# Two q loads of the second batch issued before the weights, and the last block's statistics on a turn of their own, in a retention-then-Fourier-mixing kernel

## The chip, the cores and the metric

One core of one Trainium2 chip. The metric is the device time of one execution in microseconds. TensorE (PE in the profile) does the matmuls and writes PSUM; VectorE (DVE) and ScalarE (ACT) read PSUM and do the elementwise work; GpSimd (POOL) does elementwise work on SBUF and issues the weight loads; SyncE (SP) issues all other DMAs.

## What is computed

q, k, v are 4 batches x 8 heads x 768 positions x 64, in float32. The first half is a retention recurrence with one decay per head, the second a Fourier mixing with a normalised two-layer MLP:

```python
for t in range(S):
    state = gamma * state + einsum('bhd,bhe->bhde', k[:, :, t], v[:, :, t])
    y[:, :, t] = scale * einsum('bhd,bhde->bhe', q[:, :, t], state)
x = y.transpose(0, 2, 1, 3).reshape(B, S, H * D)            # 4 x 768 x 512
u = x + real(fft(fft(x, axis=1), axis=2))
un = (u - mean(u)) / sqrt(var(u) + 1e-06)                   # over the last axis
out = u + maximum(un @ w_ch1, 0.0) @ w_ch2                  # 512 -> 2048 -> 512
```

## The kernel before, in words

**Attention.** The recurrence is done in six chunks of 128 positions, two heads (a pair) at a time, so a batch has four pairs. For each pair q, k and v come by one DMA each of 384 KB (L191, in the first batch L211) into the pool `inp` of 11 buffers. They are cast to f16 (`cast_unit`, L411: q at L423, k with its decay at L433, v at L438, on POOL). q and k are transposed on TensorE (`t_unit`, L598, tile `tq`, L615) and copied back by ACT. `a_unit` (L651) makes the products of k and q (`wkA`, L659), which DVE masks into `atm` (L662); `kv_unit` (L668) makes the states (`wkK`, then `s`, L688); `y_unit` (L694) adds state part and in-chunk part (`wkY`, L709 and L713), and ACT writes x (L721).

**Mixing.** x is folded (`fold_*`), multiplied by the tables of the first transform (`s1_unit`, L835), then of the second (`s2_unit`, L985), which gives u in six blocks of 128 rows, numbered kb: DVE at L1011 and L1014 (L1026 and L1028 in the first batch), POOL adding x at L1032 and L1034. `norm_unit` (L1038) takes the row statistics of one block: `bn_stats` (tile `bst`, L1044) and `bn_aggr` (`stats`, L1045) on DVE, then the centred copy `un` on ACT (L1046). `unT_unit` transposes `un`, on TensorE or by DMA. `rstd_unit` takes the roots (L1056, L1058).

**MLP.** It runs per batch in two halves (rt 0 and 1) of three blocks. `h_unit` (L1077) makes one of 16 rows fb of 128 hidden units: four matmuls into `psh` (L1082), one of three PSUM buffers that `psc` shares, emptied through the ReLU into `ht16` by ACT (L1086) if fb stands in `ACT_ROWS`, else by DVE (L1088). `ch_unit` (L1114) follows with 16 matmuls per block into `psc` (L1125); DVE forms the output (L1129) and SP stores it. The first batch's rt=0 uses `h0_unit` (L1099).

**The order of the work.** All engines work in order. The first batch's attention follows a list written by hand, `FIRST` (L34): each word is one unit, with its engine after `@`; `w0` to `w7` are the eight weight loads that POOL issues (L1139, L1146). The kind `long` makes fillers of f32 (L174), a matmul of zeros that only keeps TensorE going. Nine f16 fillers (L166, called at L237) stand before the list. All later work is put into streams: a list of units with a begin and an end in units of one batch; `emit` (L1249) spreads each stream's units evenly over its interval and sorts all units by time. `mix_units` (L1239) gives the streams of one half's second transform: three turns of `s2_unit`, each with the `norm_unit` of the block before, the last turn also with its own block's. The times stand in `DM0`, `DM1`, `DA0`, `DA1` (L49 to L52). For the first batch alone, POOL's order is pinned to the order of emission. Within these streams a scheduler still places the instructions of each engine.

**The loads of the second batch** stand in a stream of their own (L1291) with `after` = 6: each waits for the seventh weight load to land and for a matmul of the first batch (L193), and SP stays at the first of them until then. Their order is q, k, v pair by pair. Behind them in SP's queue come the output stores and the DMA transposes of the second batch.

Where the steps touch TensorE's program: the second batch's first transposes of q and k (L615, between psc matmuls of the first batch), the wkY matmuls at L713, and the rows of psh in the last batch.

Of the kernel before, what the change touches and what calls it, by code (L numbers as in the profile page):

```python
# [31 lines left out]
LOADS0 = [("q", 0), ("k", 0), ("q", 1), ("k", 1), ("v", 0), ("k", 2), ("v", 1), ("q", 2), ("v",  # L32
          2), ("q", 3), ("k", 3), ("v", 3)]
FIRST = """  # L34
k00@a k01@a tsa0@v ts0 xe1 tsa4@g gk1@a q0 t00 tsa2@v ts2 ta02 e00@a tsa1@g ts4 t01 tsa3@g ts1
ta00 e01@a ta10 ta22 v00@g par@v q1 gk0@g k10@v k11@a ta12 am00 am01 ta42 ta11 k20@g ae010@v
ae001@v kv0 ae000@v ae011@v t10 sc0 t11 e10@a yi01 v10@g yi00 yx0 e11@a am10 q2 x01@a am11 ts3
ta32 ta20 x00@v ta01 fl4@g ae101@v ae100@v k21@a kv1 t20 ta21 e20@a ae111@v yi11 t21 sc1
ae110@v yi10 fs0 fl2@g yx1 q3 s110 k31@g e21@a x10@v am20 am21 x11@a fs1 ta40 v22@a s010 k30@a
# [9 lines left out]
DM0, DM1 = (0.183, 0.205, 0.286, 0.408), (0.004, 0.137, 0.232, 0.341)  # L49
# [4 lines left out]
HT0 = (0.666, 0.693, 0.632, 0.590)  # L54
NPE = 2
KD = (3,)
ACT_ROWS = ((2, 5, 6, 7, 8, 9, 10, 14), (0, 3, 6, 7, 9, 10, 11, 12, 14, 15), (2, 4, 5, 6, 7, 8, 10, 14))


@with_exitstack  # L60
def kernel(
# [104 lines left out]
    def filler(n):  # L166
        def run():
            for _ in range(n):
                nc.tensor.matmul(wps, wz[:, 0:P], wz, start=True, stop=True)
        return run  # L170
# [3 lines left out]
    def filler32(n):  # L174
        def run():
            for _ in range(n):
                nc.tensor.matmul(wps[:, 0:256], wz32[:, 0:P], wz32, start=True, stop=True)
        return run

    in_of, a_of = {}, {}  # L180
    w_dma = []
    srcs = {"q": q, "k": k, "v": v}

    def load_unit(b, i, after=None):
        def run():
            h0 = 2 * PAIR_ORDER[i]
            for name, src in srcs.items():
                t = inp.tile([P, 2, NCH, D], f32, tag="in32", name=f"{name}32")
                rows = "h (p c) d -> p h c d" if b < NPE and name == "q" else \
                    "h (c p) d -> p h c d"  # L190
                dma = nc.sync.dma_start(t, src[b, h0:h0 + 2].rearrange(rows, p=P))  # L191
                if after is not None:
                    for x in (w_dma[after].ins, lb[0]["mm"].ins):  # L193
                        tc.add_manual_dep(dma.ins, x.name,
                                          mybir.DependencyInfo(mybir.DependencyClass.Sync,
                                                               mybir.DependencyReason.DATA),
                                          reason="loads in turn")
                if b > 1:
                    tc.add_manual_dep(dma.ins, a_of[b - 1, 1].ins.name,
                                      mybir.DependencyInfo(mybir.DependencyClass.Sync,  # L200
                                                           mybir.DependencyReason.DATA),
                                      reason="loads behind the transposes")
                in_of[name, b, i] = t
        return run

    def first_load(name, i, eng):
        def run():
            h0 = 2 * ORD0[i]
            t = in_of[name, 0, i] = inp.tile([P, 2, NCH, D], f32, tag="in32", name=f"{name}32")
            rows = "h (p c) d -> p h c d" if name == "q" else "h (c p) d -> p h c d"  # L210
            eng.dma_start(t, srcs[name][0, h0:h0 + 2].rearrange(rows, p=P))  # L211
        return run

    for name, i in LOADS0:
        first_load(name, i, nc.sync)()


    icol_i = const.tile([P, 8], i32, tag="icol_i")
# [15 lines left out]
    nc.gpsimd.iota(icol_i[:, 5:6], pattern=[[0, 1]], base=127, channel_multiplier=-1)  # L234
    nc.gpsimd.iota(kf_i, pattern=[[1, KN]], base=0, channel_multiplier=0)
    nc.gpsimd.memset(wz, 0.0)
    filler(9)()  # L237
    for h in range(H):
        nc.vector.memset(lgrow[:, h:h + 1], float(lng[h]))
    nc.vector.memset(maskf, 1.0)  # L240
# [148 lines left out]
    for j in range(2):  # L389
# [6 lines left out]
        t = const.tile([P, 257], f32, tag=f"qn_{j}", name=f"qn_{j}", padded_shape=[P, 260])  # L396
# [641 lines left out]
    def norm_unit(b, kb):  # L1038
        def run():
            u, stats = lb[b]["u"], lb[b]["st"]  # L1040
            bst = stt.tile([P, 6], f32, tag=f"bst{kb % 3}", name="bst")
            un = unp.tile([P, 2, 257], f16, tag="un16", name="un16").rearrange(
                "p a b -> p (a b)")[:, 0:DM]
            nc.vector.bn_stats(bst, u[:, kb, :])  # L1044
            nc.vector.bn_aggr(stats[:, kb, 0:2], bst)  # L1045
            nc.scalar.activation(un, u[:, kb, :], AF.Identity, bias=stats[:, kb, 0:1], scale=-1.0)  # L1046
            lb[b]["un", kb] = un
        return run

    def rstd_unit(b, rt):  # L1050
        def run():
            stats = lb[b]["st"]
            if b == 0 and rt == 0:
                bn_unit(0)()
            sl = slice(3 * rt, 3 * rt + 3)
            nc.scalar.activation(stats[:, sl, 2:3], stats[:, sl, 1:2], AF.Sqrt, bias=epsT,  # L1056
                                 scale=1.0)
            nc.vector.reciprocal(out=stats[:, sl, 3:4], in_=stats[:, sl, 2:3])  # L1058
        return run

    def unT_unit(b, kb):
        def run():
            un, unT = lb[b].pop(("un", kb)), lb[b]["unT"]
            if b > 1 or b and kb >= 3:
                nc.sync.dma_start_transpose(unT[:, :, kb * P:(kb + 1) * P], un)
                return
            pst = ps_g.tile([P, 4, P], f16, tag="g", name="pst", padded_shape=[P, 8, P])
            for cb in range(4):
                nc.tensor.transpose(pst[:, cb, :], un[:, cb * P:(cb + 1) * P], ident16)
            if (kb % 2 == 0) != (b == 0 and kb < 3):  # L1070
                nc.vector.tensor_copy(unT[:, :, kb * P:(kb + 1) * P], pst)
            else:
                nc.scalar.copy(unT[:, :, kb * P:(kb + 1) * P], pst)
        return run


    def h_unit(b, rt, fb):  # L1077
        def run():
            unT = lb[b]["unT"]
            psh = ps_pm.tile([P, 384], f32, tag="pm", name="psh", padded_shape=[P, DM])  # L1080
            for cb in range(4):
                nc.tensor.matmul(psh, w116[:, cb, fb * P:(fb + 1) * P],  # L1082
                                 unT[:, cb, rt * 384:(rt + 1) * 384],
                                 start=(cb == 0), stop=(cb == 3))
            if fb in ACT_ROWS[2 if (b, rt) == (B - 1, 0) else rt]:
                nc.scalar.activation(ht16[:, fb, :], psh, AF.Relu, bias=0.0, scale=-1.0)  # L1086
# [149 lines left out]
                    s=s1b_unit, sa=sa_unit, bn=bn_unit, pt=pt0_unit,  # L1236
                    gr=gr_unit, xe=x_edges)[kind](*n)

    def mix_units(b, kbs):  # L1239
        def turn(j):  # L1240
            def run():
                if j < len(kbs):
                    s2_unit(b, kbs[j])()
                for n in kbs[max(j - 1, 0):j] + (kbs[-1:] if j == len(kbs) - 1 else []):
                    norm_unit(b, n)()
            return run
        return [turn(j) for j in range(len(kbs))], [unT_unit(b, kb) for kb in kbs]

    def emit(streams):  # L1249
        ev = []  # L1250
# [18 lines left out]
    streams = []  # L1269
    for b in range(B):  # L1270
        majors = []
        if b == 0:
            for kb in range(3):
                if kb:
                    majors.append(unT_unit(0, kb))
                majors += [h0_unit(kb, g) for g in range(4)]
        else:
            majors += [h_unit(b, 0, fb) for fb in range(NFB)]
        majors.append(rstd_unit(b, 0))
        majors += [ch_unit(b, 0, rb3, part) for rb3 in range(3) for part in range(4)]  # L1280
# [3 lines left out]
        s2s, unTs = mix_units(b, [3, 4, 5])  # L1284
        dm = DM0 if b == 0 else DM1
        streams += [(majors, b, b + 1.0), (s2s, b + dm[0], b + dm[1]),
                    (unTs, b + dm[2], b + dm[3])]
        if b + 1 < B:
            steps = attn_steps(b + 1)
            if b == 0:  # L1290
                streams.append(([load_unit(1, i, 6) for i in range(4)], LD0[0], LD0[1]))  # L1291
                streams.append(([qt_zeros], 0.1, 0.15))
                streams.append(([half_tables], HT0[0], HT0[1]))
                streams.append(([pad_unit], HT0[2], HT0[3]))
                ts = TS0
            else:
                streams.append(([load_unit(b + 1, i) for i in range(4)], b + LD1[0], b + LD1[1]))
                n = [len(u) for u in steps[1:]]
                ts = list(TS1[:2]) + [TS1[2] + TS1[3] * sum(n[:j]) / sum(n) for j in range(6)]
# [6 lines left out]
            s2s, unTs = mix_units(b + 1, [0, 1, 2])  # L1306
            streams += [(s2s, end + da[2], end + da[3]), (unTs, end + da[4], end + da[5])]
    emit(streams)


# [28 lines left out]
```

## Time and profile before

| | |
|---|---|
| median of 3 runs | 245.32 us (245.0 to 245.47) |
| the profiled execution | 245.19 us |
| its span, first to last instruction | 243.1 us |
| TensorE busy | 230.3 us (95%) |
| VectorE, ScalarE, GpSimd busy | 173.6, 120.7, 83.3 us |
| mean granted TensorE clock | 0.986 |
| moved by DMA | 36.59 MB, mean 151 GB/s |
| 16 loads each of q, k, v | 384 KB each, about 6 us to landing |
| 8 weight loads, cast to f16 on the way | 512 KB each as stored, 11.3 us to landing |

The time of the profiled execution is the span and about 2 us around it. A timeline row is: start, duration, engine, line and operation, output<-input, shape, count, and in brackets the idle time before it with what ended it. Where rows are merged, the duration is that of the group. Matmul ends are modelled: rows of TensorE overlap, so the starts say more than the ends. PEld rows are its weight loads. A row of stretches has the stretch, its length, the busy time (and count) of PE, PEld, DVE, ACT and POOL, the granted clock as a share of full speed, the DMA share (in these rows the mean over the 16 engines can read above 1, since packets overlap) and GB/s.

### The profile page before, as it was taken

The page shows a single profiled execution, that of the slowest core. Times are in us where ns is not written, and L with a number is a line of the kernel's source. Part 1 is how long each engine was busy: PE and PEld are TensorE (multiplying, and loading weights), DVE is VectorE, ACT ScalarE, POOL GpSimd, SP SyncE. Part 2 cuts the span into 40 slices and gives each one's busy share as a digit, 9 for nine tenths or more (in the row PEclk, how much of TensorE's full clock was granted, in tenths as well). Part 3 has the DMA queues.
Part 4 walks back from the last instruction along what each step waited for, and adds up shares of the span by engine and source line. Part 5 has one row for each costly group of instructions (what it writes and reads, how often), then busy time and mean ns, then how long its engine had stood idle before and what let it go on. Part 6 is the DMA issues. An engine that isn't in the chain of part 4 may idle for free.

```text
span 243.1 us, 5251 instructions
## 1 busy us (share of the span) xinstructions
PE 230.3 (95%) x2005; PEld 144.3 (59%) x2005; DVE 173.6 (71%) x423; ACT 120.7 (50%) x267; POOL 83.3 (34%) x151
## 2 busy tenths in 40 slices
PE   6399999989999999999999999899999999999994
PEld 1376679756865646665557446555675455446543
DVE  8979987947997889986985749977886557414121
ACT  5989758665865444841248406722356316203400
POOL 7678802356500097850001808920003214000000
PEclk9769999999999999999999999999999999999999
DMA  7996999999989859999999588775100230221012
GB/s 184 229 271 103 203 206 194 234 225 255 279 184 226 155 123 242 175 186 141 266 273 215 102 176 183 157 109 151 46 0 0 75 122 23 43 89 43 1 43 89
DMA packets 100009, 36.59 MB, mean 151 GB/s; under 512 B 90640, under 2 KB 97040, under 8 KB 99984
## 3 DMA queue, kind: packets, MB, share of 16 engines
q1 hardware_dynamic: 95760, 32.06, 63.3%
q0 software_dynamic: 4224, 4.19, 10.7%
q8 instruction: 16, 0.26, 0.5%
q14 instruction: 9, 0.07, 0.1%
HBM read 27.26 MB, written 6.29 MB: 138 GB/s over the span
## 4 chain that ended last, share of the span: by engine, by line
PE 68%; DVE 13%; DMA 5%; ACT 4%; POOL 4%; issue 2%; SPq 1%; POOLq 0%; ACTq 0%; DVEq 0%
PE psc L1125 32%; PE psh L1082 21%; DMA v<-in_v_dram 3%; PE ps L842 3%; PE wkA L659 2%; DMA k<-in_k_dram 2%; DVE atm L662 2%; DVE bst L1044 2%; PE wkY L713 2%; DVE u L1011 2%; POOL u L1032 1%; POOL u L1034 1%; DVE ht L1088 1%; PE ps L822 1%; PE pq L916 1%
## 5 line engine op out<-in xcount | busy, mean ns | idle before, releaser
L1125 PE MATMUL psc<-w,ht 128*128 128x512 f16 (+2 forms) x400 | 88.9, 370 | 0.0
L1082 PE MATMUL psh<-unT,w 128*128 128x384 f16 x448 | 81.8, 326 | 0.5 <-ACT ht L1086 0.3
L1125 PEld LDWEIGHTS <-ht 128*128 128x128 f16 x400 | 37.6, 98 | 36.8
L1082 PEld LDWEIGHTS <-w 128*128 128x128 f16 x448 | 42.3, 98 | 24.9 <-issue 1.9
L1086 ACT ACTIVATE ht<-psh 128x384 f16<-128x384 f32 x64 | 30.9, 490 | 42.2 <-PE psh L1082 41.5
L1032 POOL TENSOR_TENSOR u<-u,x 128x256 f32<-128x256 f32 x21 | 13.3, 635 | 105.7 <-DVE u L1011 93.3
L1129 DVE SCALAR_TENSOR_TENSOR ob<-psc,stats,u 128x512 f32<-128x512 f32 (+2 forms) x25 | 18.1, 725 | 29.6 <-PE psc L1125 29.5
L1088 DVE TENSOR_SCALAR ht<-psh 128x384 f16<-128x384 f32 x48 | 26.3, 550 | 8.9 <-PE psh L1082 8.3
L662 DVE TENSOR_TENSOR atm<-wkA,maskp 128x512 f16<-128x512 f32 x36 | 23.6, 680 | 1.7 <-PE wkA L659 1.6
L1046 ACT ACTIVATE un<-u,stats 128x512 f16<-128x512 f32 x21 | 14.7, 720 | 13.4 <-DVE stats L1045 8.5
L1044 DVE BATCH_NORM_STATS2 bst<-u 128x6 f32<-128x512 f32 x21 | 14.5, 691 | 5.6 <-POOL u L1034 5.4
L688 DVE SCALAR_TENSOR_TENSOR s<-s,gk,wkK 128x128 f16<-128x128 f16 x48 | 16.2, 337 | 2.6 <-ACT s L684 1.8
L721 ACT ACTIVATE x<-wkY,gexp 128x384 f16<-128x384 f32 x24 | 12.6, 579 | 8.9 <-PE wkY L713 8.9
L433 POOL TENSOR_SCALAR kd<-k,gexp 128x384 f16<-128x384 f32 x24 | 13.8, 585 | 3.3 <-DMA k<-in_k_dram 3.3
L659 PE MATMUL wkA<-qTz,kT 128*128 128x256 f16 x72 | 13.4, 272 | 0.0
L1034 POOL TENSOR_TENSOR u<-u,x 128x256 f32<-128x256 f32 x21 | 13.3, 635 | 0.0
L1006 ACT COPY qn<-pq 128x128 f32<-128x128 f32 x18 | 4.9, 274 | 14.0 <-PE pq L1004 13.9
L1099 PEld LDWEIGHTS <-w 128*128 128x128 f16 x192 | 11.0, 98 | 0.8 <-issue 0.3
L1099 PE MATMUL psh<-unT,w 128*128 128x128 f16 x192 | 11.4, 219 | 0.1
L1011 DVE SCALAR_TENSOR_TENSOR u<-pq,g,qn 128x256 f32<-128x256 f32 x18 | 8.5, 474 | 3.3 <-PE psh L1082 2.5
L438 POOL TENSOR_SCALAR v<-v 128x768 f16<-128x768 f32 x12 | 10.0, 831 | 1.1 <-DMA v<-in_v_dram 1.1
L659 PEld LDWEIGHTS <-kT 128*128 128x128 f16 x72 | 6.9, 98 | 5.6 <-issue 0.4
(177 smaller groups left out, 315.0 us busy)
## 6 DMA issues: line engine op xcount, KB each, us to landing
q<-in_q_dram SPq DMA_DIRECT2D x16, 384.0 KB, 6.0
k<-in_k_dram SPq DMA_DIRECT2D x16, 384.0 KB, 5.8
v<-in_v_dram SPq DMA_DIRECT2D x16, 384.0 KB, 6.2
out_dram<-ob SPq DMA_DIRECT2D x23, 256.0 KB, 2.8
w<-in_moe_w_ch_dram POOLq DMA_DIRECT2D x8, 512.0 KB, 11.3
unT<-un SPq DMA_TRANSPOSE x15, 2.4
out_dram<-ob SPq DMA_DIRECT2D x1, 192.0 KB, 1.9
kT<-kd SPq DMA_TRANSPOSE x9, 3.2
```

The source lines that it names most:

```text
L659: mm = nc.tensor.matmul(wk[:, c2], st["kT"][:, c, :], st["qT"][:, :, c, :], start=True, stop=True)
L662: nc.vector.tensor_tensor(out=st["atm"][:, 2 * part:2 * part + 2], in0=wk, in1=maskp[:, PAIR_ORDER[i]].unsqueeze(1).to_broadcast([P, 2, 2, ...
L688: nc.vector.scalar_tensor_tensor(out=s16[:, c], in0=s16[:, c - 1], scalar=gk2[:, hp:hp + 1], in1=wk[:, c - c0], op0=ALU.mult, op1=ALU.add)
L1032: nc.gpsimd.tensor_tensor(out=u[:, kb, 0:256], in0=u[:, kb, 0:256], in1=x[:, kb, 0, 1:257], op=ALU.add)
L1034: nc.gpsimd.tensor_tensor(out=u[:, kb, 256:512], in0=u[:, kb, 256:512], in1=x[:, kb, 1, 257:1:-1], op=ALU.add)
L1044: nc.vector.bn_stats(bst, u[:, kb, :])
L1082: nc.tensor.matmul(psh, w116[:, cb, fb * P:(fb + 1) * P], unT[:, cb, rt * 384:(rt + 1) * 384], start=(cb == 0), stop=(cb == 3))
L1086: nc.scalar.activation(ht16[:, fb, :], psh, AF.Relu, bias=0.0, scale=-1.0)
L1088: nc.vector.tensor_scalar(out=ht16[:, fb, :], in0=psh, scalar1=-1.0, scalar2=0.0, op0=ALU.mult, op1=ALU.max)
L1099: mm = nc.tensor.matmul(psh[:, f], w116[:, cb, fb * P:(fb + 1) * P], unT[:, cb, kb * P:(kb + 1) * P], start=(cb == 0), stop=(cb == 3))
L1125: nc.tensor.matmul(psc[:, c0:c1], ht16[:, fb, rb3 * P:(rb3 + 1) * P], w216[:, fb, c0:c1], start=(fb == 0), stop=(fb == NFB - 1))
L1129: nc.vector.scalar_tensor_tensor(out=ob[:, c0:c1], in0=psc[:, c0:c1], scalar=lb[b]["st"][:, rb, 3:4], in1=lb[b]["u"][:, rb, c0:c1], op0=AL ...
```

## The change

Four edits stand in the diff. The q loads of the second batch's first two pairs are issued directly behind the first batch's loads, with no wait on the weights; the later stream skips what is already loaded. The fillers change in kind and place: four f32 and one f16 filler instead of nine f16 ones, and the word `long2` twice in `FIRST`. `mix_units` returns three streams instead of two: the third block's `norm_unit` gets a time of its own, a share `NT` of a turn behind the last `s2_unit`. In the last batch's rt=0 the rows 11 and 13 move from DVE to ACT.

```diff
-k00@a ... tsa1@g ts4 t01 tsa3@g ts1
-ta00 e01@a ta10 ta22 v00@g par@v q1 gk0@g k10@v k11@a ta12 am00 am01 ta42 ta11 k20@g ae010@v
+k00@a ... tsa1@g ts4 t01 long2 tsa3@g ts1
+ta00 e01@a ta10 ta22 v00@g par@v q1 gk0@g k10@v k11@a ta12 am00 am01 long2 ta42 ta11 k20@g ae010@v
...
-ACT_ROWS = ((2, 5, 6, 7, 8, 9, 10, 14), (0, 3, ...), (2, 4, 5, 6, 7, 8, 10, 14))
+NT = 0.6
+ACT_ROWS = ((2, 5, 6, 7, 8, 9, 10, 14), (0, 3, ...), (2, 4, 5, 6, 7, 8, 10, 11, 13, 14))
...
-    def load_unit(b, i, after=None):
+    def load_unit(b, i, after=None, names="qkv"):
         def run():
             h0 = 2 * PAIR_ORDER[i]
-            for name, src in srcs.items():
+            for name in names:
+                if (name, b, i) in in_of:
+                    continue
+                src = srcs[name]
...
     for name, i in LOADS0:
         first_load(name, i, nc.sync)()
+    load_unit(1, 0, None, "q")()
+    load_unit(1, 1, None, "q")()
...
-    filler(9)()
+    filler32(4)()
+    filler(1)()
...
-    def mix_units(b, kbs):
+    def mix_units(b, kbs, s0, s1, u0, u1):
         def turn(j):
             def run():
-                if j < len(kbs):
-                    s2_unit(b, kbs[j])()
-                for n in kbs[max(j - 1, 0):j] + (kbs[-1:] if j == len(kbs) - 1 else []):
-                    norm_unit(b, n)()
+                s2_unit(b, kbs[j])()
+                if j:
+                    norm_unit(b, kbs[j - 1])()
             return run
-        return [turn(j) for j in range(len(kbs))], [unT_unit(b, kb) for kb in kbs]
+        t = s1 + NT * min((s1 - s0) / 3, u1 - s1)
+        return [([turn(j) for j in range(3)], s0, s1), ([norm_unit(b, kbs[2])], t, t),
+                ([unT_unit(b, kb) for kb in kbs], u0, u1)]
```

`emit`'s callers pass the same times as before. In the built program the changes of order are these. SP: the two q loads stand 13th and 14th, and a few loads of the third batch move past an output store or a DMA transpose. TensorE: the fillers, and at one place four wkY matmuls ahead of one psh matmul instead of behind it. DVE: the statistics of the third block behind one `atm` at two places, and two ReLU evictions fewer. ACT: at the same two places one x copy between the last two `un` copies, and the two ReLU evictions. POOL's order is the same.

More of the change, by code (lines that the diff above doesn't have):

```diff
@@ L34 @@
 FIRST = """
-k00@a k01@a tsa0@v ts0 xe1 tsa4@g gk1@a q0 t00 tsa2@v ts2 ta02 e00@a tsa1@g ts4 t01 tsa3@g ts1
-ta00 e01@a ta10 ta22 v00@g par@v q1 gk0@g k10@v k11@a ta12 am00 am01 ta42 ta11 k20@g ae010@v
+k00@a k01@a tsa0@v ts0 xe1 tsa4@g gk1@a q0 t00 tsa2@v ts2 ta02 e00@a tsa1@g ts4 t01 long2 tsa3@g ts1
+ta00 e01@a ta10 ta22 v00@g par@v q1 gk0@g k10@v k11@a ta12 am00 am01 long2 ta42 ta11 k20@g ae010@v
 ae001@v kv0 ae000@v ae011@v t10 sc0 t11 e10@a yi01 v10@g yi00 yx0 e11@a am10 q2 x01@a am11 ts3
@@ L56 @@
 KD = (3,)
-ACT_ROWS = ((2, 5, 6, 7, 8, 9, 10, 14), (0, 3, 6, 7, 9, 10, 11, 12, 14, 15), (2, 4, 5, 6, 7, 8, 10, 14))
+NT = 0.6
+ACT_ROWS = ((2, 5, 6, 7, 8, 9, 10, 14), (0, 3, 6, 7, 9, 10, 11, 12, 14, 15), (2, 4, 5, 6, 7, 8, 10, 11, 13, 14))
 @with_exitstack
@@ L1283 @@
         majors += [ch_unit(b, 1, rb3, part) for rb3 in range(3) for part in range(4)]
[L1284 to L1287, printed above, removed]
+        streams.append((majors, b, b + 1.0))
+        streams += mix_units(b, [3, 4, 5], *(b + t for t in (DM0 if b == 0 else DM1)))
         if b + 1 < B:
@@ L1305 @@
                              if cb or b + 1 >= FB], end + da[0], end + da[1]))
-            s2s, unTs = mix_units(b + 1, [0, 1, 2])
-            streams += [(s2s, end + da[2], end + da[3]), (unTs, end + da[4], end + da[5])]
+            streams += mix_units(b + 1, [0, 1, 2], *(end + t for t in da[2:]))
     emit(streams)
```

## The prediction

> **What bounds the kernel now.** I read the page's first part, then the waits of TensorE, then the timeline around each wait, engine by engine.
>
> ```profile
> span 243.1 us, 5251 instructions
> PE 230.3 (95%) x2005; PEld 144.3 (59%) x2005; DVE 173.6 (71%) x423; ACT 120.7 (50%) x267; POOL 83.3 (34%) x151
> ```
>
> TensorE is busy for 95% of the span, so only its own gaps can be won. Its waits from 36 us on (line, releaser: us in total, times, longest):
>
> ```profile
> PE wkY L713 <- DVE atm L662: 0.8, 2, 0.7
> PE tq L615 <- POOL kd L433: 0.8, 1, 0.8
> PE psh L1082 <- ACT ht L1086: 0.3, 1, 0.3
> PE psh L1082 <- DVE ht L1088: 0.2, 1, 0.2
> ```
>
> Five stops, 2.1 us. These are idle times after modelled ends. Two back-to-back groups, quoted first in the next fence, start 0.34 us apart though each is shown as 0.50 long, so a stop really costs the distance of starts less 0.34/6 = 0.056 us per 128-column transpose. I use distances of starts, with 0.163 us for a 384-column matmul (207.10 to 208.40 for eight, quoted further down) and 0.029 for the wkY ones (101.45 to 101.74 for ten).
>
> **The change part by part.**
>
> **1. Two q loads go ahead of the weights.** The stop is at the second batch's first pair:
>
> ```profile
> 56.30 0.50 PE L615 MATMUL tq<-ident,q16z 128*128 128x128 f16 x6
> 56.64 0.50 PE L615 MATMUL tq<-ident,kd 128*128 128x128 f16 x6
> ...
> 44.04 0.37 SPq L191 DMA_DIRECT2D q<-in_q_dram  x1
> 44.50 0.42 SPq L191 DMA_DIRECT2D k<-in_k_dram  x1
> ...
> 49.06 0.83 POOL L423 TENSOR_SCALAR q16z<-q 128x768 f16<-128x768 f32 x1 [3.72 <-PE pst L1069]
> 50.53 0.50 PE L615 MATMUL tq<-ident,q16z 128*128 128x128 f16 x6
> 50.57 1.15 POOL L433 TENSOR_SCALAR kd<-k,gexp 128x384 f16<-128x384 f32 x2 [0.69 <-DMA k<-in_k_dram]
> 51.78 0.51 PE L615 MATMUL tq<-ident,kd 128*128 128x128 f16 x6 [0.76 <-POOL kd L433]
> ```
>
> TensorE is through the q transposes at 50.53 + 0.34 = 50.87 and starts the k transposes at 51.78: 0.91 us lost. It waits for the casts of k, which wait for k's landing at about 50.5. The q cast at 49.06 is put down to a TensorE transpose, but the transpose whose count it waits for is of the first batch and long done; it waited for q's landing, 5.0 us after the issue.
>
> With q loaded early, POOL casts q as soon as it is through with the u adds ahead of it, and k(1,0) is the first load issued at 44.04 instead of the second. How long it then takes is not shown; the bounds are q's 5.0 us (landing 49.05) and k's own 6.0 us (50.05). Neither end is right: k moves in smaller pieces than q but has none ahead. I take the middle, 49.55. The k casts then end at 49.55 + 1.15 = 50.70 and TensorE can go on at 50.76, before it is ready (50.87). So the whole 0.91 goes; at the late end (50.05) TensorE waits until 51.28 and 0.50 goes. I take 0.80. Cover: q(1,1) is cast from a tile that is there; k and v of later pairs land one or two q transfers earlier.
>
> SP issues these loads as its 13th and 14th, straight behind the last v. Their only waits are for the first batch's v and k loads and for casts that POOL and ACT finished in the first 13 us, so nothing is queued behind a long wait. What the two take on the DMA engines is the question. Stretches of the span, with the last columns granted clock, DMA share, GB/s:
>
> ```profile
> 20.00:20.50 0.50, 0.50 (x10) 0.48 (x7) 0.50 (x3) 0.50 (x3) 0.38 (x1) 1.00 1.28 220
> 20.50:21.00 0.50, 0.50 (x9) 0.37 (x6) 0.50 (x3) 0.50 (x2) 0.50 (x2) 1.00 0.69 111
> 22.50:23.00 0.50, 0.36 (x9) 0.27 (x10) 0.50 (x1) 0.50 (x3) 0.49 (x2) 1.00 0.00 0
> 23.00:23.50 0.50, 0.50 (x16) 0.45 (x16) 0.50 (x2) 0.50 (x2) 0.47 (x2) 1.00 0.33 18
> ```
>
> The input loads end at about 20.8, and at 23.0 to 23.5 the weights, issued by POOL from 21.6 on, still move only 18 GB/s. Between lies a hole of at least 2.7 us. A q load is 0.39 MB; at 220 GB/s that is 1.8 us, at the 340 GB/s of the best stretch below 1.2 us. Two take 2.4 to 3.6 us: the hole holds them, or all but 0.9 us.
>
> ```profile
> 3.00:4.00 1.00, 1.00 (x4) 0.43 (x3) 0.96 (x5) 0.51 (x3) 0.66 (x8) 1.00 1.13 340
> ```
>
> Call the weights' delay d. The SP queue waits for the seventh weight before it issues k(1,0), so d comes straight onto the 44.04 above. I take d = 0.1 (the loads of q, in long rows, are nearest to the 340), which leaves the 0.80 as it is; ends 0 and 3.6.
>
> The Trainium skill (DMA: Bandwidth & Descriptors, Issuing engines are not separate DMA queues) speaks against this edit: DMAs started by different engines run on the same 16 DMA engines and interleave. By that, two q loads in flight beside the weights would cost the weights their full 2.4 us. The row of 22.5 to 23.0 shows nothing to interleave with; the rule bites only on what sticks out of the hole.
>
> **2. Fillers at the start.** Eight of the nine 128x512 f16 fillers become four 128x256 f32 ones, and two f32 ones go behind the first k transposes and two behind the first wkA products.
>
> ```profile
> 2.15 3.84 PE L169 MATMUL wps<-ht 128*128 128x512 f16 x9 [2.15 <-POOL ht L236]
> 9.79 0.82 PE L517 MATMUL wkA<-qTz,kT 64*128 64x128 f16 x12 [2.04 <-ACT kT L503]
> 11.67 0.75 PE L545 MATMUL wkK<-v,kd 128*64 128x64 f16 x10 [1.06 <-POOL v L474]
> ```
>
> A f16 filler takes 3.84/9 = 0.43 us. No f32 matmul is in the trace: by half the columns 0.21, by four times the f16 one's 1.7; I take 0.85, at which the first block is as long as before. Two then take 1.7 us: inside the 2.04 us wait before wkA, but 0.64 over the 1.06 us before wkK. The Trainium skill (FP8 and Floating Point Precision, TensorE Precision Notes) says that true FP32 takes four passes; an estimate by that is four times 256 columns, also 0.85.
>
> What starts late there does not last. The granted clock (the column before the DMA share) is at half until just before 16 us:
>
> ```profile
> 14.00:16.00 2.00, 1.75 (x33) 1.30 (x30) 0.93 (x2) 1.73 (x5) 1.27 (x2) 0.52 1.24 281
> 16.00:18.00 2.00, 1.82 (x36) 1.42 (x31) 2.00 (x5) 2.00 (x5) 2.00 (x3) 1.00 1.15 294
> ```
>
> If the fillers keep it up, TensorE's 1.75 us of matmuls in 14 to 16 us, and as many in the stretch before, take half as long, and by the engines behind them I put the saving at no more than 1 us; if not, up to 0.6 is lost. Neither reaches the end whole: the weights land on their own schedule (the fourth, issued last at 25.6, takes 10.4 us: 36.0, and TensorE uses it at 36.2), and k lands by the weights. So a gain is capped at about 0.1, and a loss is eaten by VectorE's idle 1.07 us of 14 to 16. I put the start at 0, with -0.1 to +0.6.
>
> ```profile
> L1139 POOL DMA_DIRECT2D w<-in_moe_w_ch_dram x4: 747/774/994, 21.6 to 25.6; - x4
> DMA to landing us min/median/max: 6.7/8.4/10.4
> 36.23 1.05 PE L1099 MATMUL psh<-unT,w 128*128 128x128 f16 x16
> ```
>
> **3. The last block's statistics on a turn of their own.** On VectorE the built order differs in two places only, during rt=0 of the batches b = 1 and 2: bst, bst, aggr, atm, aggr, s becomes bst, atm, aggr, bst, s, aggr. Before, at the second place and the first:
>
> ```profile
> 152.83 0.69 DVE L1044 BATCH_NORM_STATS2 bst<-u 128x6 f32<-128x512 f32 x1
> 153.87 0.69 DVE L1044 BATCH_NORM_STATS2 bst<-u 128x6 f32<-128x512 f32 x1 [0.35 <-POOL u L1034]
> 154.56 0.66 DVE L662 TENSOR_TENSOR atm<-wkA,maskp 128x512 f16<-128x512 f32 x1
> ...
> 154.30 0.33 PE L1082 MATMUL psh<-unT,w 128*128 128x384 f16 x1
> 155.27 0.29 PE L713 MATMUL wkY<-v,atm 128*128 128x64 f16 x4 [0.65 <-DVE atm L662]
> ...
> 101.45 0.45 PE L709 MATMUL wkY<-s,qTz 128*128 128x64 f16 x10
> 101.74 0.28 PE L713 MATMUL wkY<-v,atm 128*128 128x64 f16 x4
> 102.21 0.41 PE L713 MATMUL wkY<-v,atm 128*128 128x64 f16 x8 [0.19 <-DVE atm L662]
> ```
>
> The second bst waits for POOL's u, and atm, whose products are long there, stands behind it. Moved ahead, atm runs from 153.52 to 154.18, and the four wkY matmuls can follow at 154.30. TensorE's stop of 155.27 - 154.30 - 0.16 = 0.81 goes. At 102 the stop is 102.21 - 101.74 - 4 x 0.029 = 0.35 and goes likewise. What is late next is bst, hence un and its transpose, by about 0.4 us on VectorE and one x cast on ACT (0.58, the L721 group's mean on the page): covered by rt=0's psc stage, 48 matmuls that come before rt=1 needs unT. Bounds: all (1.16), or nothing if the psh evictions, which VectorE does in between, only take over the wait. VectorE loses its own 0.35 wait, so I take 1.1.
>
> **4. Rows 11 and 13 of the last batch's rt=0 to ACT.**
>
> ```profile
> 202.87 4.06 PE L1082 MATMUL psh<-unT,w 128*128 128x384 f16 x24 [0.26 <-ACT ht L1086]
> 207.10 1.46 PE L1082 MATMUL psh<-unT,w 128*128 128x384 f16 x8 [0.17 <-DVE ht L1088]
> 208.40 0.38 PE L1125 MATMUL psc<-w,ht 128*128 128x512 f16 x1
> ...
> 205.54 0.47 ACT L1086 ACTIVATE ht<-psh 128x384 f16<-128x384 f32 x1
> 206.69 0.72 ACT L1046 ACTIVATE un<-u,stats 128x512 f16<-128x512 f32 x1 [0.68 <-issue]
> ```
>
> The stop is 207.10 - 202.87 - 24 x 0.163 = 0.32: fb 14 needs the buffer of fb 11, which VectorE empties only behind its last bst. In the new order ACT empties it right behind fb 10, at 206.0 to 206.5, in its own idle time. fb 13 goes behind un (0.72) and a short root, ends near 208.1, and the first psc takes its buffer just then. I take 0.25 (0 to 0.32).
>
> **Sum.** 0.80 + 0 + 1.1 + 0.25 = 2.15 us. The profiled execution took 245.19 us (span 243.1 and 2.1 around it), the median of the three runs is 245.32, so the profile stands within 0.1% of it. 245.19 - 2.15 = 243.0 us.
>
> **The rivals.**
>
> - **The weights come late (slower).** If the q loads run beside the weights rather than in the hole, k is issued at 44.04 + d and the time is 243.0 + d - 0.1 from d = 0.1 on. At 2.4 us it is 245.3, no change; it is slower by more than 0.2% from d = 2.8, and at 3.6, two loads at 220 GB/s with none of the hole, 246.5. For it: POOL issues from 21.6, and TensorE has only 0.2 us in hand at 36.2. Against it: the empty stretches, and two loads fit them. 0.14 for slower by this, 0.10 for a d around 2 that leaves the time as it is.
> - **Half of it only.** k lands at its late end, and psh evictions take the place of the atm waits: 245.19 - 0.50 - 0.35 - 0.17 = 244.2 (243.9 to 244.7). For it: five waits lie on three engines that are 34 to 71% busy with work in fixed order. Chance 0.18.
> - **The q loads don't come early at all**, held on SP by a buffer: then the weights and k stay where they are and 245.19 - 1.35 = 243.8. The waits that SP has before them are over before 16 us; 0.03, counted as faster.
> - **The f32 fillers are dear**: 1.7 us each with a clock that stays at half would put wkK at 18 us instead of 11.67. Against: the clock rises in a busy stretch by 16 us at the latest. 0.02, slower.
>
> **How the numbers follow.** The forecast has 0.53 and a range of its own of 242.6 to 243.7. Faster by over 0.2% (0.5 us, about what a measurement of this kernel can tell from no change): 0.53 + 0.18 + 0.03 = 0.74; within 0.2%: 0.10; slower: 0.14 + 0.02 = 0.16. The range from 242.5 (start gains its 0.1, all stops go in full) to 245.3 (d = 2.4) leaves out the slower cases and little else.
>
> **What would show it.** In the profile after: no TensorE wait for kd near 51 us, the q cast well before 49 us, the first k cast before 50; DMA share in 21 to 23 us near 1 and the seventh weight still landing at about 44; no TensorE waits for atm; and the wait for VectorE's ht in the last batch gone. Wrong I would be if the issue of k moved from 44 to 46 us or later, or if TensorE came to the L1099 row of 36.2 us over 0.5 us late.

## The result, and the profile after

The changed kernel takes 243.81 us (median of 6 runs, 243.6 to 244.57), the kernel before 245.5 us (6 runs, 245.0 to 246.6). The ratio is 0.9932, with a 95% interval of 0.9913 to 0.9951: faster by 0.7%. The profiled execution took 243.74 us, 1.45 less than that of before; 2.15 were forecast.

The first part of the page, with the clock row and the instruction queue further down:

```profile
span 241.6 us, 5268 instructions
PE 229.7 (95%) x2013; PEld 145.6 (60%) x2013; DVE 173.3 (72%) x421; ACT 121.3 (50%) x269; POOL 83.0 (34%) x151
...
PEclk9999999999999999999999999999999999999999
...
q8 instruction: 16, 0.26, 0.5%
```

The clock row no longer shows the dip of before, half speed from about 9 to 16 us. It isn't at full speed from the very start: the trace's first record of the clock begins at 5.34 us, the row reads full where there is no record, and the fillers ahead of it ran slowly (last section). The queue row will be needed: 16 blocks of 16 KB, 0.26 MB, are read by DMA during the run. They are put down to TensorE's program because they come all along its work, 101 to 155 matmuls apart.

TensorE's waits from 36 us to the end (releaser: us in total, times, longest). Of five stops one is left, the one that the change doesn't touch:

```profile
PE psh L1089 <- ACT ht L1093: 0.3, 1, 0.3
```

So the four stops that the change was made to remove are gone. The timeline at the four places (L622 was L615, L720 was L713, L1089 was L1082, L1132 was L1125):

```profile
45.14 0.37 SPq L195 DMA_DIRECT2D k<-in_k_dram  x1
...
46.43 0.83 POOL L430 TENSOR_SCALAR q16z<-q 128x768 f16<-128x768 f32 x1
49.63 1.15 POOL L440 TENSOR_SCALAR kd<-k,gexp 128x384 f16<-128x384 f32 x2 [2.38 <-DMA k<-in_k_dram]
...
51.64 0.50 PE L622 MATMUL tq<-ident,q16z 128*128 128x128 f16 x6
51.97 0.50 PE L622 MATMUL tq<-ident,kd 128*128 128x128 f16 x6
...
101.92 0.51 PE L720 MATMUL wkY<-v,atm 128*128 128x64 f16 x12
...
153.75 0.51 PE L720 MATMUL wkY<-v,atm 128*128 128x64 f16 x12
154.10 1.46 PE L1089 MATMUL psh<-unT,w 128*128 128x384 f16 x8
155.40 0.38 PE L666 MATMUL wkA<-qTz,kT 128*128 128x256 f16 x2
...
201.74 5.36 PE L1089 MATMUL psh<-unT,w 128*128 128x384 f16 x32 [0.26 <-ACT ht L1093]
206.94 0.38 PE L1132 MATMUL psc<-w,ht 128*128 128x512 f16 x1
```

The starts of q and k transposes are 0.33 us apart, the matmuls at L720 run as one group, and the last rows of psh run without the stop at 207.

But the start is late. The first batch's psh, which began at 33.01 us before, and what stands ahead of it:

```profile
20.50:21.00 0.50, 0.00 (x0) 0.00 (x0) 0.50 (x2) 0.00 (x0) 0.00 (x0) 1.00 0.71 112
21.00:21.50 0.50, 0.00 (x0) 0.00 (x0) 0.50 (x2) 0.15 (x1) 0.09 (x1) 1.00 0.56 118
21.50:22.00 0.50, 0.00 (x0) 0.00 (x0) 0.20 (x1) 0.50 (x2) 0.50 (x2) 1.00 0.96 252
```

```profile
21.41 0.59 POOL L469 TENSOR_SCALAR kd<-k,gexp 128x384 f16<-128x384 f32 x1 [2.15 <-DMA k<-in_k_dram]
...
22.11 0.50 PE L498 MATMUL tq<-ident,kd 128*128 128x128 f16 x6 [1.65 <-POOL kd L469]
...
22.76 1.75 POOL L1146 DMA_DIRECT2D w<-in_moe_w_ch_dram  x2
...
34.11 3.00 PE L1106 MATMUL psh<-unT,w 128*128 128x128 f16 x48
...
37.33 1.05 PE L1106 MATMUL psh<-unT,w 128*128 128x128 f16 x16
```

In the stretches (busy times of PE, PEld, DVE, ACT, POOL), TensorE, ACT and POOL all stand still from 20.5 to 21 us. They wait for k of the first batch's last pair, the load before the last, called k(0,3) below. It is issued at 13.79 us, as before, and lands at 21.33; before it landed at 20.04. TensorE starts its transposes late, and POOL issues the weights, which stand behind its cast of k in its order, 1.1 us late (22.76 for 21.65). The last row is the one that the prediction named as a sign of being wrong if it came over 0.5 us late: it began at 36.23 before, so it is 1.10 late.

The same places in the timeline of before, with one more matmul that the next table uses:

```profile
20.12 0.76 POOL L462 TENSOR_SCALAR kd<-k,gexp 128x384 f16<-128x384 f32 x1 [0.65 <-DMA k<-in_k_dram]
...
33.01 3.00 PE L1099 MATMUL psh<-unT,w 128*128 128x128 f16 x48
...
156.54 0.38 PE L659 MATMUL wkA<-qTz,kT 128*128 128x256 f16 x2
```

The time saved so far, as the start of the same matmuls before less that after, adds up as follows:

```
first psh of the first batch   33.01 -  34.11 = -1.10
kd transposes of batch 1       51.78 -  51.97 = -0.19   +0.91 (q loads)
wkA behind the second atm     156.54 - 155.40 = +1.14   +1.33 (turns)
first psc of the last batch   208.40 - 206.94 = +1.46   +0.32 (rows)
```

The gains behind the start are 2.56 us, and 1.10 of them are lost at the start.

### The profile page after: what moved, and what is told of

Read it like the earlier page. It is cut to its first block, busy times and chain, and to the rows that moved or that the text cites. A ratio compares the mean times of both kernels' runs of the same rounds, so it can differ in the third digit from the quotient of the medians.

```text
span 241.6 us, 5268 instructions
## 1 busy us (share of the span) xinstructions
PE 229.7 (95%) x2013; PEld 145.6 (60%) x2013; DVE 173.3 (72%) x421; ACT 121.3 (50%) x269; POOL 83.0 (34%) x151
## 4 chain that ended last, share of the span: by engine, by line
PE 82%; SPq 5%; DVE 5%; DMA 3%; ACT 1%; issue 1%; POOL 1%; ACTq 0%; DVEq 0%
PE psc L1132 34%; PE psh L1089 28%; SPq L215 5%; PE psh L1106 3%; DMA k<-in_k_dram 3%; PE wkA L666 3%; PE ps L849 3%; PE wkY L720 2%; PE pq L1011 2%; PE ps L829 1%; PE wkY L716 1%; PE wkK L685 1%; PE pq L923 1%; PE tq L622 1%; DVE atm L669 1%
## 5 line engine op out<-in xcount | busy, mean ns | idle before, releaser
L1132 PE MATMUL psc<-w,ht 128*128 128x512 f16 (+2 forms) x400 | 88.9, 370 | 0.0
L1089 PE MATMUL psh<-unT,w 128*128 128x384 f16 x448 | 81.5, 326 | 0.3 <-ACT ht L1093 0.3
L1132 PEld LDWEIGHTS <-ht 128*128 128x128 f16 x400 | 37.6, 98 | 36.7
L1089 PEld LDWEIGHTS <-w 128*128 128x128 f16 x448 | 42.3, 98 | 24.6 <-issue 1.5
L1093 ACT ACTIVATE ht<-psh 128x384 f16<-128x384 f32 x66 | 31.7, 490 | 41.0 <-PE psh L1089 40.2
L1095 DVE TENSOR_SCALAR ht<-psh 128x384 f16<-128x384 f32 x46 | 25.3, 549 | 9.1 <-PE psh L1089 8.7
```

The lines of the kernel that those rows point to most:

```text
L1089: nc.tensor.matmul(psh, w116[:, cb, fb * P:(fb + 1) * P], unT[:, cb, rt * 384:(rt + 1) * 384], start=(cb == 0), stop=(cb == 3))
L1095: nc.vector.tensor_scalar(out=ht16[:, fb, :], in0=psh, scalar1=-1.0, scalar2=0.0, op0=ALU.mult, op1=ALU.max)
L1132: nc.tensor.matmul(psc[:, c0:c1], ht16[:, fb, rb3 * P:(rb3 + 1) * P], w216[:, fb, c0:c1], start=(fb == 0), stop=(fb == NFB - 1))
```

## The experiments

**The question** is what makes k(0,3) late. In the trace a load's arrival is recorded in 16 parts, and it counts as landed with the last of them. Of k(0,3), 15 parts arrive by 19.96 in both kernels; the last comes at 20.04 before and at 21.33 after. Of the load behind it, the last v, 15 parts arrive by 21.5 in both, and the last at 22.44 before and 22.49 after. So in both kernels one part of 16 falls behind the others: before, it does so from this v on, and after the change one load earlier, from k(0,3) on. The trace also shows each read of TensorE's program: 16 KB in one packet, the first during the span at 19.10 before (1.30 us long) and at 17.95 after (1.25 us long). In both it comes when TensorE has started 135 matmuls (127 to 141 in all the kernels below), and after the change TensorE is there 1.15 us earlier. The faster clock is about half of that: the 126th matmul that isn't a filler starts at 19.05 before and at 18.46 after. The other half is the fillers' number: they are 17 records of TensorE in place of 9, so the 135th matmul is now the 118th that does work.

**Theory A:** the fillers bring the fetch forward, into the time of k(0,3), and it holds up one sixteenth of that load. **Theory B:** the two q loads, queued behind the last v, delay k(0,3).

The Trainium skill (Runtime: NRT & Kernel Launch, Instruction fetch mechanics) says that an engine's program is refilled in blocks of 16 KiB, 256 instructions, over a DMA queue of its own, and that the cost of crossing a boundary is mostly hidden. The 16 packets of queue q8 agree with the size: 2013 matmuls with a weight load each are 4026 instructions, an estimate of 15.7 blocks by that page. By its last sentence A would be worth about nothing. The runs decide against that here: TensorE works on through the fetch, but a load that it needs later is held up.

All runs in one table. "Fetch" is the start of the first fetch; "15 and 16" the arrival of the 15th and of the 16th, last part of the first batch's last load but one, which is k(0,3), or v(0,2) in e10 to e12, where the order of loads is another; "start" the first psh of the first batch. All of these are from the profiled run, the median and ratio (to the runs of before on the same chip) from all. The experiments ran on several chips, on which the kernel before took 245.0 to 245.5 us, so a difference of medians between two rows can be off by a few tenths of a us.

```
                      fetch   15 and 16        start   median   ratio [95%]
before                19.10   19.96  20.04    33.01   245.50
after                 17.95   19.96  21.33    34.11   243.81   0.9932 [0.9913, 0.9951]
e1  late q            18.37   20.01  21.33    34.11   245.05   0.9993 [0.9973, 1.0012]
e2  old fillers       18.85   20.05  20.10    33.12   242.72   0.9906 [0.9884, 0.9929]
e3  fillers only      18.25   20.07  21.42    34.20   246.79   1.0076 [1.0050, 1.0102]
e4  old turns         18.26   20.24  21.21    33.99   244.93   0.9981 [0.9966, 0.9995]
e5  old rows          18.08   19.93  21.37    34.16   244.09   0.9955 [0.9936, 0.9974]
e6  early fetch       16.35   19.98  21.47    34.25   243.86   0.9946 [0.9925, 0.9966]
e7  wide fillers      19.26   20.04  20.13    33.14   242.95   0.9898 [0.9865, 0.9930]
e8  fewer of them     19.22   20.02  20.16    33.15   242.86   0.9893 [0.9870, 0.9915]
e9  early q only      19.09   20.01  20.10    33.10   244.58   0.9966 [0.9950, 0.9983]
e10 order of loads    19.21   19.98  20.08    33.49   243.37   0.9918 [0.9889, 0.9947]
e11 same, new fillers 17.83   19.95  21.33    33.67   243.24   0.9909 [0.9887, 0.9932]
e12 v cast earlier    19.20   20.07  20.23    35.50   243.25   0.9917 [0.9898, 0.9937]
```

### e1: the q loads back at their place

```diff
-    load_unit(1, 0, None, "q")()
-    load_unit(1, 1, None, "q")()
```

> The changed kernel with the two q loads of the second batch back at their old place behind the weights; its fillers, turns and rows stay. Theory A (the fillers keep the clock up, TensorE comes 1.15 us earlier to the point at which 16 KB of its program are fetched, and that fetch holds up one DMA engine's share of k of the last pair): k of that pair still lands at 21.3 us, the weights are still issued from 22.8, the start (first psh of L1106, 34.11 in the changed kernel, 33.01 before) stays at 34.1, and the stop before the second batch's kd transposes is back: 243.8 + 0.9 = 244.7 us. Theory B (the two q loads behind the last v delay that k): k lands at 20.0, the weights are issued from 21.65, the start is at 33.0, and the time is 243.8 - 1.1 + 0.9 = 243.6.

Measured: 245.05 us. The timeline of e1:

```profile
21.42 0.58 POOL L467 TENSOR_SCALAR kd<-k,gexp 128x384 f16<-128x384 f32 x1 [2.12 <-DMA k<-in_k_dram]
...
34.11 3.00 PE L1104 MATMUL psh<-unT,w 128*128 128x128 f16 x48
...
51.64 0.50 PE L620 MATMUL tq<-ident,q16z 128*128 128x128 f16 x6
52.45 0.51 PE L620 MATMUL tq<-ident,kd 128*128 128x128 f16 x6 [0.31 <-POOL kd L438]
...
118.71 0.38 PE L664 MATMUL wkA<-qTz,kT 128*128 128x256 f16 x2 [0.53 <-DMA qTz<-q16z]
```

Without the q loads k(0,3) is just as late: theory B falls. The stop of the second batch is back with 0.81 - 0.34 = 0.47 us, less than the 0.91 of before, and a new one of 0.53 us for a DMA transpose stands in the third batch, so the total of 1.24 us is above the 0.9 expected; the two stops account for 1.00 of it.

### e2: the old fillers

```diff
-... ts4 t01 long2 tsa3@g ... am01 long2 ta42 ...
+... ts4 t01 tsa3@g ... am01 ta42 ...
-    filler32(4)()
-    filler(1)()
+    filler(9)()
```

> The changed kernel with the nine f16 fillers of before and no others; early q loads, turns and rows stay. Theory A: the fetch of TensorE's program is back at 19.1 us, k of the last pair lands at 20.0, the weights are issued from 21.65, the first psh of the first batch starts at 33.0, and the time is 243.8 - 1.1 = 242.7 us. Theory B: k lands at 21.3, the start stays at 34.1 or is later, and the time is 243.8 or a little more.

Measured: 242.72 us, the lowest median here, though e7 and e8 can't be told from it by their ratios. All four runs lie below the fastest of the changed kernel. The timeline of e2:

```profile
20.19 0.82 POOL L468 TENSOR_SCALAR kd<-k,gexp 128x384 f16<-128x384 f32 x1 [0.67 <-DMA k<-in_k_dram]
...
21.24 0.49 PE L497 MATMUL tq<-ident,kd 128*128 128x128 f16 x6 [0.16 <-ACT kd L466]
...
21.77 1.75 POOL L1145 DMA_DIRECT2D w<-in_moe_w_ch_dram  x2
...
33.12 3.00 PE L1105 MATMUL psh<-unT,w 128*128 128x128 f16 x48
```

With the q loads in place k lands at 20.10. So the fillers alone cost the changed kernel about 1.1 us: 1.09 by the medians, 0.99 by the start of psh.

### e3: the new fillers alone

The kernel before, with the three lines of e2's diff the other way round.

> The kernel before with the new fillers alone. Theory A: the fetch at 17.95 us, k of the last pair lands at 21.3, the weights are issued from 22.8, the first psh starts at 34.1, and all of the old stops stand: 245.4 + 1.1 = 246.5 us. Theory B: k lands at 20.0 and the start is at 33.0 or earlier: 245.4 or up to 0.5 less.

Measured: 246.79 us, 1.48 above the kernel before on that chip. Of that, 1.19 is the start (34.20 for 33.01), as A has it; a further stop of 0.4 us before a later group of kd transposes comes on top. So the new fillers, with nothing else, make the kernel slower.

### e6: the fetch still earlier

```diff
     filler(1)()
+    for _ in range(20):
+        nc.tensor.matmul(wps[:, 0:16], wz[:, 0:P], wz[:, 0:16], start=True, stop=True)
```

> The changed kernel with 20 matmuls of 16 columns more behind the first fillers, which TensorE does in its idle time ahead of the first transposes and whose results nobody reads. They move every later instruction of TensorE 20 places back in its program. Theory A: the fetch comes about 20 matmuls earlier in the work, at 16 to 17.5 us; it then holds up one DMA engine's share of the last pair's q too, which lands at about 19.4 in place of 18.25, and k still lands at about 21.3: time 243.8, at most 0.5 more. Theory B and any other that has no part for the fetch: q lands at 18.25, k at 21.3, time 243.8.

Measured: 243.86 us, against 242.72 for e2 on the same chip, with no run of one in the range of the other. The fetch is at 16.35, 1.60 us earlier than in the changed kernel, and the last part of the last pair's q now arrives at 19.73 in place of 18.25, with 15 parts there by 18.20. The timeline of e6:

```profile
20.79 0.51 PE L500 MATMUL tq<-ident,q16z 128*128 128x128 f16 x6 [0.69 <-POOL q16z L457]
22.25 0.49 PE L500 MATMUL tq<-ident,kd 128*128 128x128 f16 x6 [0.95 <-POOL kd L471]
```

Twenty matmuls that nobody needs move a load's landing by 1.48 us. The fetch's place follows from the place in TensorE's program, and the load that is late follows from the fetch.

### e7 and e8: fewer instructions for the fillers

```diff
-                nc.tensor.matmul(wps[:, 0:256], wz32[:, 0:P], wz32, ...)
+                nc.tensor.matmul(wps, wz32[:, 0:P], wz32.unsqueeze(1).to_broadcast([P, 2, 256]), ...)
-    filler32(4)()
-    filler(1)()
+    filler32(2)()
```

In `FIRST`, each `long2` becomes `long1`. In e8 the start has `filler32(1)()`, and the second `long` is gone.

> The changed kernel with f32 fillers of 512 columns in place of pairs of 256 ones and without the one f16 filler: the same filler time to within 0.4 us in 8 records instead of 17, so that what follows stands 9 places earlier in TensorE's program. Theory A: with the clock up, the fetch comes 9 matmuls later in the work, near 18.4 us. A fetch at 18.25 and 18.37 us held up k of the last pair, one at 18.85 didn't, so here it is on the edge: either k at 21.3 and 243.8 us as in the changed kernel, or k at 20.0 and 242.5. Theory B: no difference, 243.8.

> As the one with wide fillers, with just one wide filler at the start and one behind the first k transposes: 4 records instead of 17, 13 places. Theory A, if the clock stays up: the fetch comes near 18.8 us, k of the last pair lands at 20.0, TensorE waits for its casts until 20.8 at most, the start is at 32.7 to 33.0 and the time is 242.3 to 242.7 us. If the clock falls back to half, as before the change, the fetch is at about 19.5 and the time is that of the f16 fillers, 242.7. Theory B: 243.8.

Measured: 242.95 and 242.86 us. In both the fetch comes at about 19.2 us, k at 20.15, the start at 33.15. For e7 the fetch was expected near 18.4; it is later than that, since the granted clock fell just then. Stretches of e7:

```profile
14.00:16.00 2.00, 1.31 (x28) 0.68 (x22) 1.66 (x4) 2.00 (x5) 1.27 (x2) 1.00 1.24 279
16.00:18.00 2.00, 1.54 (x18) 1.55 (x19) 2.00 (x4) 1.99 (x4) 2.00 (x3) 0.62 1.15 295
18.00:20.00 2.00, 2.00 (x27) 1.47 (x24) 1.45 (x4) 1.83 (x5) 0.99 (x2) 0.53 1.35 226
```

In e8 the trace's first record of a full clock begins at 15.83 us. So neither profiled run gives what was wanted, a clock at full speed up to a late fetch, and what the faster clock alone does to k(0,3), without the 8 further places, is not shown. But e7 has the fast clock up to 16 us and half of it from there, e2 half the clock from 10 to 16 us, and they start the psh at 33.14 and 33.12: the clock at the start is worth nothing here, because TensorE waits for k in any case.

### e4: the old turns

```diff
                 s2_unit(b, kbs[j])()
-                if j:
-                    norm_unit(b, kbs[j - 1])()
+                for n in kbs[max(j - 1, 0):j] + (kbs[-1:] if j == 2 else []):
+                    norm_unit(b, n)()
```

The stream with the third `norm_unit` goes.

> The changed kernel with the last block's norm unit back in the last turn of mix_units; the rest of the change stays. By the sum of the prediction (both atm stops, 0.35 and 0.81 by starts): TensorE stands for VectorE's atm near 102 and 154 us again and the time is 243.8 + 1.1 = 244.9 us, 0.8 to 1.2 above. Rival (what is late next takes the place of the stops, so that the edit is worth half or less): 244.0 to 244.4.

Measured: 244.93 us, 1.12 above the changed kernel. The timeline of e4 has both stops again:

```profile
102.29 0.41 PE L720 MATMUL wkY<-v,atm 128*128 128x64 f16 x8 [0.19 <-DVE atm L669]
...
154.24 0.33 PE L1089 MATMUL psh<-unT,w 128*128 128x384 f16 x1
155.21 0.29 PE L720 MATMUL wkY<-v,atm 128*128 128x64 f16 x4 [0.65 <-DVE atm L669]
```

### e5: the old rows

```diff
-ACT_ROWS = (..., (2, 4, 5, 6, 7, 8, 10, 11, 13, 14))
+ACT_ROWS = (..., (2, 4, 5, 6, 7, 8, 10, 14))
```

> The changed kernel with rows 11 and 13 of the last batch's rt=0 back on VectorE. By the sum of the prediction: the stop before fb 14's buffer near 206 us is back, 0.25 to 0.32 us, 244.1. Rival (VectorE, whose last bst now stands elsewhere, empties fb 11 in time): 243.8 and no stop.

Measured: 244.09 us, 0.28 above the changed kernel, which alone would be inside the spread of the runs. The timeline of e5 has the stop, 206.03 - 201.81 - 24 x 0.163 = 0.31 us:

```profile
201.81 4.06 PE L1089 MATMUL psh<-unT,w 128*128 128x384 f16 x24 [0.26 <-ACT ht L1093]
206.03 1.46 PE L1089 MATMUL psh<-unT,w 128*128 128x384 f16 x8 [0.17 <-DVE ht L1095]
```

### e9: the early q loads alone

The kernel before, with the changed `load_unit` and its two early calls.

> The kernel before with the two early q loads alone; fillers, turns and rows as before. Theory A with the sum of the prediction: k of the last pair lands at 20.0 us, the weights are issued from 21.65, the start is at 33.0, the stop before the second batch's kd transposes goes, 0.8 to 0.9 us: 245.4 - 0.85 = 244.55. Theory B: k lands at 21.3, the start is 1.1 later, and the time is 245.6.

Measured: 244.58 us, 0.92 below before. Timeline and stretches of e9:

```profile
43.79 0.37 SPq L194 DMA_DIRECT2D k<-in_k_dram  x1
...
50.64 0.50 PE L620 MATMUL tq<-ident,q16z 128*128 128x128 f16 x6
50.98 0.50 PE L620 MATMUL tq<-ident,kd 128*128 128x128 f16 x6
```

```profile
21.00:21.50 0.50, 0.31 (x7) 0.23 (x5) 0.50 (x3) 0.50 (x2) 0.50 (x2) 1.00 1.03 287
21.50:22.00 0.50, 0.50 (x16) 0.40 (x13) 0.50 (x3) 0.50 (x2) 0.50 (x2) 1.00 1.14 345
...
22.50:23.00 0.50, 0.29 (x7) 0.19 (x8) 0.50 (x1) 0.50 (x3) 0.49 (x2) 1.00 0.99 363
```

The two loads fill the hole from 21 to 23 us, at 287 to 363 GB/s, and the next k is issued at 43.79, no later than the first load of that batch before (44.04): the weights lose nothing.

### e10, e11, e12: another victim for the fetch

```diff
-LOADS0 = [..., ("v", 2), ("q", 3), ("k", 3), ("v", 3)]
+LOADS0 = [..., ("q", 3), ("k", 3), ("v", 2), ("v", 3)]
-... ta40 v22@a s010 k30@a t30 e30@a t31 ...
+... ta40 s010 k30@a t30 e30@a v22@a t31 ...
```

e10 has the fillers of e2, e11 those of the changed kernel. e12 is e10 with `v22@a` directly behind `k30@a`.

> The changed kernel with the f16 fillers, and with the v of the third pair loaded behind the last pair's q and k (its cast on ScalarE moves behind the kd one). q and k of the last pair then land one load earlier, near 16.5 and 18.25 us, v of the third near 20.0. By the trace of the same kernel without this, TensorE is ready for the kd transposes at 20.93 and starts them at 21.24: at most 0.3 us less, 242.4 to 242.7 us. If the start is bound elsewhere (the chain through the casts), 242.7.

> The same order of loads with the changed kernel's own fillers. Theory A: the fetch at about 18 us now falls on the third pair's v, which lands at 21.3 in place of 20.0 and is needed later than k was; k of the last pair lands near 18.25, TensorE does the kd transposes near 20.4 and stands for v's cast until about 22.0 in place of 22.5: 243.2 us, 0.3 to 0.8 below the changed kernel. If the fetch has no part in it, k at 18.25 frees the whole 1.1 us and more: 242.4.

Measured: e11 243.24 us, as A has it. The fetch at 17.83 now holds up v(0,2), whose last part arrives at 21.33 with 15 parts there by 19.95; k lands at 18.25. e10 missed, with 243.37 us against 242.4 to 242.7. The timeline of e10:

```profile
21.03 0.49 PE L497 MATMUL tq<-ident,kd 128*128 128x128 f16 x6
21.50 0.36 PE L551 MATMUL wkK<-v,kd 128*64 128x64 f16 x6
22.42 0.30 PE L551 MATMUL wkK<-v,kd 128*64 128x64 f16 x4 [0.56 <-ACT v L483]
```

TensorE is 0.2 us earlier, and then stands for a cast of v that the edit had put behind a copy of 0.80 us on ACT.

> As the changed kernel with f16 fillers and the third pair's v loaded last but one, with that v's cast on ScalarE directly behind the kd cast, ahead of the copy of the transposed q, where the former version had it behind. That version started the kd transposes at 21.03 us (21.24 with the old order of loads) and then lost 0.59 us in the wkK matmuls to this cast. Here the cast runs at about 20.6 to 21.1, TensorE doesn't wait, the start is at 32.9 and the time is 242.5 us, 0.2 below the version with the old order of loads. If the chain through the casts binds in some other place, 242.7 or more.

Measured: 243.25 us (242.51 to 245.14 in 7 runs). The wait for that cast is gone; the profiled run is the slowest of the seven, with the granted clock at 0.50 from 26 to 28 us, and its late start of 35.50 is no use as evidence. Whether this order beats e2 is not shown.

## Why the prediction was right, and where it was off

Its forecast was 243.0, its range 242.5 to 245.3. The sign held, and so did the mechanisms of three parts of four. That the time stayed in the range is in part luck: a loss of 1.1 us that the sum put at nothing was made up by 0.4 us more from the other parts than forecast (2.56 by starts, against 2.15) and by a range that reached far up for another reason, weights delayed by the q loads. One of its two signs of being wrong came true, the L1099 row, 1.10 us late with 0.5 allowed; the other, an issue of k at 46 us or later, did not (45.14).

1. **The q loads (0.80):** right, 0.91 by starts and 0.92 in e9. k landed 4.4 us after its issue, 0.6 below the lower bound taken, so its casts were done ahead of need. The hole holds both loads (e9). It was not quite as empty as read: the input loads did not all end at 20.8, since one part of the last v came until 22.44, but at 4 to 18 GB/s that took next to nothing of it. The rule of the Trainium skill that was weighed there (DMA: Bandwidth & Descriptors, Issuing engines are not separate DMA queues) says that DMAs share the same 16 engines whoever starts them; the prediction took 2.4 us from it as the price for the weights. In e9 the first load behind them was issued 0.25 us earlier, not later, as there was nothing in the hole to interleave with.
2. **The fillers (0, with -0.1 to +0.6):** this is the step that failed. Its price of a f32 filler was right: 3.55 us for the four at the start, or 0.89 each, for 0.85 taken. So was the reason that a faster TensorE gains nothing at the start. What failed is the term of 0 itself: for fillers that keep the clock up it allowed a gain of at most 0.1 us and no loss, and a loss of up to 0.6 only if they didn't. They did keep it up, and the start came 1.1 us late. The premise behind the term, that the weights land on their own schedule, is the error: POOL issues them behind its cast of k(0,3), whose landing hangs on TensorE through the fetch of its program. e2 and e3 show the cost from both sides (0.99 and 1.19 us by starts), e6 to e8 and e11 show that the fetch is the link.
3. **The turns (1.1):** right, 1.12 in e4; 1.33 by the ledger above, of which 0.35 + 0.81 are the two stops.
4. **The rows (0.25):** right, 0.32 by starts and 0.28 in e5.

With the start where it was before, the forecast would have been 0.3 too high: e2, which is just that, takes 242.72. The rival "the weights come late" was right that the weights could be issued late (22.76 for 21.65), and wrong on the cause: it put them behind the q loads, and they stood behind the cast of a late k.

What stays open: the packets in the trace don't name their DMA engine. That the held part of the load and the fetch were on the same one is inferred from 16 parts of which one is late, by 1.0 to 1.5 us where the fetch takes 1.2 to 1.3, in each of the seven kernels whose fetch comes by 18.37 us (the last v behind it then has a late part too), while in the seven with a fetch from 18.85 us on the lateness begins with that last v. The packets themselves bear this out. From 18.4 to 20.4 us the trace has 21.3 to 21.6 load packets in flight on average while no fetch runs, and 20.0 to 20.2 while one does, one sixteenth less, in all kernels but e6, whose fetch lies earlier. And in the kernel before, while only the late part of v is out (21.5 to 22.3 us), its packets of 256 B come singly, one every 14 ns, as from one engine. Why 18.85 is late enough, though 1.2 us of fetch then still end at the time of the landing, was not tried; that this engine had by then taken on its share of k is only an argument.

## What to carry to other kernels

A stage that waits for a load gains nothing from a faster engine, and can lose. Here TensorE's place in its program decided when its next block of program was fetched, and that fetch took DMA time from the loads in flight. A faster clock and additional instructions, even ones that only fill time, both bring the fetch forward. Where a load lands about a microsecond late without more traffic, compare the arrival of its 16 parts and look at the instruction queue. An edit with several parts deserves a run without each part: here three parts gained some 2.6 us (e2 against the kernel before on its chip) and the fourth gave 1.1 back.

## What the runs showed of the hardware

- One fetch of 16 KB of program took 1.2 to 1.3 us between 16 and 21 us, with loads in flight. When it began by 18.37 us, one of the 16 parts of a 384 KB load, the first batch's last but one, came 1.0 to 1.5 us behind the others. It went by the count of instructions: 20 matmuls more ahead of it brought it from 17.95 to 16.35 us.
- An f32 matmul of 128x256 (two records each in the profile) took 0.89 us at the start and 0.54 us once the clock was up. The changed kernel's first four fillers, and the next two:

```profile
2.15 3.55 PE L178 MATMUL wps<-ht 128*128 128x256 f32 x8 [2.15 <-POOL ht L242]
...
7.58 1.08 PE L178 MATMUL wps<-ht 128*128 128x256 f32 x4
```

- A granted clock of 1.00 on the page can mean that the trace has no record of it yet. In e8 the stretches read 1.00 from 2 to 20 us, but the first record begins at 15.83 us. Six transposes took 0.82 us at 6 us, as in the kernel before with 0.50 granted (12.47 us), and 0.51 from 16.6 us on:

```profile
6.12 0.82 PE L498 MATMUL tq<-ident,q16z 128*128 128x128 f16 x6 [1.90 <-POOL q16z L455]
...
16.58 0.51 PE L498 MATMUL tq<-ident,q16z 128*128 128x128 f16 x6
```
